# Idle products in planned gaps of the TensorE queue, with new planner constants, in a delta-rule attention and gated MLP kernel

## The chip, the cores and the metric

The kernel runs on one core of a Trainium2 chip. The metric is the device time of one execution in microseconds (us), as a median over runs. A profile is one execution, recorded instruction by instruction. Its engines are PE (TensorE matmul), PEld (TensorE weight load), DVE (VectorE), ACT (ScalarE), POOL (GpSimd) and SP (SyncE, whose queue issues the DMAs).

## What is computed

Three layers follow each other, all in float32 for a batch of 4 with 768 tokens: delta-rule attention over 8 heads of 48, a convolution-gated projection, and an MLP with a product over the tokens.

```python
for t in range(S):                                   # attention, state per head 48 x 48
    y[:, :, t] = einsum('bhd,bhde->bhe', q[:, :, t], state)
    v_old = einsum('bhde,bhd->bhe', state, kt)
    state = state + bt * einsum('bhd,bhe->bhde', kt, vt - v_old)
gate = sigmoid(causal depthwise conv of x, 5 taps)   # first gated layer, 384 wide
x = (gate * (x @ w_val)) @ w_out
h = gelu(x @ w_in); u, v = halves of h               # second layer, 1024 wide
v_s = einsum('ts,bsd->btd', w_sg, layernorm(v) * g_ln) + b_sg
out = x + (u * v_s) @ w_out2
```

## The kernel before

**Tiling.** The sequence is cut into 48 chunks of 64 tokens, 12 for each batch entry. `norm`, `keys`, `gram`, `base` and `merge` prepare the keys and the triangular inverses of sets of chunks; `base` is a recursion of some sixty small DVE operations for a set of eight chunks (tiles `X`, `tmp`). `seq(n)` carries the state through chunk n: PE forms `ps_q` and `ps_state`, and ACT and DVE read them back as pairs of float16 halves (`wh`). `attend(n)` forms the outputs (`ps_y`, `mh`, `ys`), which go to DRAM as `xd`. The MLP runs over tiles of 256 tokens: `front` (convolution, tile `a`), `value`, `hidden` (with the layer norm), `gates`, `mix`, `final`. Its PSUM banks are named `ps_mlp`. Nearly every product is three float16 products of halves. `load_weights`, `load_weights2` and `load_weights3` split the weights into halves on the chip, with exact float32 loads through the tile `wst` and float32 products with the identity `eye`.

**The order.** No loop writes the instruction order. Every call is recorded as an `Op` (which is why all instructions bear one line, L109), and `Program.in_order` then places all of them by list scheduling: it keeps a planned time for each engine, and lets each take, of the operations whose inputs are planned to be ready, the one with the highest weight. The weight is the length of the chain behind an operation, scaled by engine by the table `CHAIN`, plus an offset by stage (`STAGE`) and a term for its due chunk. The durations that the planner assumes come from `cost`. On the chip every engine then works through its queue strictly in the planned order, each instruction waiting on semaphores for its inputs. An instruction that stands early in a queue and has to wait holds up all behind it.

**TensorE in the planner.** `PE_WINDOW` and `PE_BUSY` say when the planner believes that TensorE runs at half clock; then it charges n / 1200 us for n columns in place of n / 2400. A product of a 64 x 64 block is charged at least 0.0255 us, and a change between blocks and full products `PE_CHANGE`.

**PSUM.** All eight banks are in use: `ps_a` one, `ps_m` three, and one each for `ps_b`, `ps_y`, `ps_q` and `ps_state`. The state uses 192 of the 512 columns of its bank.

Of the kernel before, what the change touches and what calls it, by code (L numbers as in the profile page):

```python
# [3 lines left out]

# [7 lines left out]
F32 = mybir.dt.float32  # L12
# [5 lines left out]
DRAM = bass.MemoryType.DRAM  # L18
# [3 lines left out]
class Op:  # L22


    def __init__(self, index, engine, method, call, kw):
        self.index, self.engine, self.method, self.call, self.kw = index, engine, method, call, kw
        self.before, self.after, self.stage, self.due = set(), [], None, 0
        self.ready = 0.0
        self.cost, self.time, self.port = cost(self)
        self.blocks = engine == "tensor" and kw["lhsT"].shape[0] == kw["lhsT"].shape[1] == 64  # L30


class Memory:
# [6 lines left out]
class Program:  # L40
# [7 lines left out]

    def __init__(self, tc):
        self.tc, self.ops, self.memory, self.masks, self.first = tc, [], {}, {}, []  # L50
        self.stage, self.due = None, 0
# [59 lines left out]
    def in_order(self):  # L111
        for op, m in self.first:
            op.before |= m.users
        for op in self.ops:
            assert all(o.index < op.index for o in op.before)
            op.left = len(op.before)
            for o in op.before:
                o.after.append(op)
        for op in reversed(self.ops):
            weight, wait = CHAIN[op.engine]  # L120
            op.chain = max((o.chain + (wait if o.engine != op.engine else 0.0) for o in op.after), default=0.0)
            op.chain += weight * (op.time + (op.cost + DMA_LATENCY + DMA_SEMAPHORE + reads(op) if op.engine == "sync" else 0.0))
# [12 lines left out]
        blocks = False  # L135

        def finish(op):
            for o in op.after:
                if o.engine != op.engine:
                    t = op.end + LATENCY[op.engine]  # L140
                elif op.engine == "tensor":
                    t = op.start
                else:
                    t = op.end + (LATENCY[op.engine] if op.engine == "sync" else 0.025)
                o.ready = max(o.ready, t)
                o.left -= 1
                if not o.left:
                    heappush(later[o.engine], (o.ready, o.index, o))

        while len(done) < len(self.ops) or waiting:  # L150
            t, e = min(((free[e] if now[e] else max(free[e], later[e][0][0]), i) for i, e in enumerate(ENGINES)
                        if (now[e] or later[e]) and not (waiting and e == "gpsimd")), default=(1e9, 0))
            if waiting and t >= held["vector"] + 0.02:
                op, waiting = waiting, None
                t = max(op.start, held["vector"])
                op.end = held["gpsimd"] = t + op.time
                free["gpsimd"] = t + op.cost
                finish(op)
                continue
# [19 lines left out]
            if e == "tensor" and op.blocks != blocks:  # L179
                blocks = op.blocks  # L180
                t += PE_CHANGE
            if e in ("vector", "scalar"):
                if e in last and drains(last[e], op):
                    t = max(t, last[e].start + last[e].time)
                last[e] = op
            op.start, used, time = t, op.cost, op.time
            done.append(op)
            if e == "vector":
                if op.port:
                    wait = max(0.0, held["gpsimd"] - t - 0.1)  # L190
                    wait += PORT_WAIT if wait > 0 else 0.0
                    used, time = used + wait, time + wait
                    held[e] = t + time - 0.05
            elif e == "gpsimd":
                if held["vector"] > t:
                    waiting = op
                    continue
                held[e] = t + time - 0.04
            elif e == "tensor":

                window, n = int(t / PE_WINDOW), int(np.prod(op.kw["out"].shape[1:])) * (mybir.dt.size(op.kw["rhs"].dtype) // 2) ** 2
                if busy.get(window - 1, 0) < PE_BUSY:
                    used = max(used, n / 1200)
                    time = max(time, used + 0.2)
                busy[window] = busy.get(window, 0) + n
# [7 lines left out]
            finish(op)  # L213
        return sorted(done, key=lambda op: (op.start, op.index))


# [33 lines left out]

DMA_QUEUE, DMA_SEMAPHORE = 8, 0.79

PE_WINDOW, PE_BUSY = 4096 / 1200, 3060

PE_CHANGE = 0.12

PORT_WAIT = 0.3

CHAIN = dict(tensor=(0.304, 0.508), scalar=(0.543, 0.071), vector=(2.092, 0.024), gpsimd=(2.017, 0.416), sync=(2.173, 0.387))


LATER = ("front", "value", "hidden", "gates", "mix", "final", "front0", "value0", "hidden0", "gates0", "mix0", "final0")
# [1 line left out]
DUE = dict(first=0.1, later=0.0534)  # L264


STAGE = dict(merge0=-0.2223, mix=0.3267, mix0=0.0197, gram0=-0.1735, load_weights2=-0.1156, seq0=0.0455, base0=0.0794, front0=0.1721, norm0=0.0229, load_weights3=0.0206, gates0=-0.0831, attend0=-0.0259, load_weights=0.0123)


def cost(op):  # L270
# [8 lines left out]
    far = n > 64 and any(step(a) > 8 for a in ins)  # L279
    if engine == "tensor":  # L280
        n *= 4 if mybir.dt.size(op.kw["rhs"].dtype) == 4 else 1
        t = max(0.0255, n / 1200 + 0.006 if step(op.kw["rhs"]) > 1 else n / 2400 + 0.0015)
        return t, t + 0.165, False
    if engine == "scalar":
        if apart:
# [4 lines left out]
        elif size == 4 and out.shape[0] == 32:  # L290
            t = 0.37
# [39 lines left out]

def reads(op):

    return DMA_READ if op.kw["in_"].space == DRAM else 0.0


def drains(op, after):

    p, q = (o.kw["out"].start_partition() for o in (op, after))
    return p != q and not (p < q and max(o.kw["out"].shape[0] for o in (op, after)) <= 64)  # L340


def step(ap):
# [15 lines left out]
def kernel(  # L359
# [150 lines left out]
    for x, t in [(0.0, eye32)] + [(x, const.tile([P, 128], F16, name=f"minus{i}")) for i, x in enumerate((1.0, SWG))]:  # L510
        nc.gpsimd.memset(t, 0.0)
        nc.gpsimd.affine_select(out=t, in_=t, pattern=[[1, 128]], compare_op=ALU.not_equal, fill=-1.0 / x if x else 1.0,
                                base=0, channel_multiplier=-1)
        minus[x] = t

    def hl_left(dst_hi, dst_lo, src, scale):

# [235 lines left out]
    def seq(n):  # L753
# [19 lines left out]
        hl_psum(we[:, 0], we[:, 1], pw, 1.0 / ST)  # L773
        if c < NC - 1:
            if c == 0:
                state["ps"] = ps_1.tile([P, PR, E], F32, name="ps_state", tag="s")
            pst = state["ps"]
            mmh(lambda h: pst[:, h, :], lambda x, h: kbd[x][:, h], lambda y, h: we[:, y, h], c == 0)
            hl_psum(we[0:EP, 2], we[0:EP, 3], pst[0:EP], 1.0 / SK)
# [415 lines left out]
```

## Time and profile before

| | |
|---|---|
| runs | 701.59, 702.41 and 706.77 us; median 702.41 us |
| profiled execution | 699.62 us; its span, from the first to the last instruction, is 697.9 us |
| busy in that span | PE 570.3 us (82%), DVE 529.2 (76%), ACT 400.6 (57%), POOL 175.1 (25%) |
| TensorE clock granted | mean 0.938 of full |

The span is read in stages, since the busy shares are averages over parts with different limits. Up to about 190 us the weights are split and the first eight chunks are worked; from there to 600 us the chunks and the MLP of earlier batch entries run side by side; in the last 98 us only the MLP of the last entry is left. Matmuls are pipelined and a busy PE is not one at its peak.

### The profile page before, as it was taken

What the parts mean: (1) busy time and instruction counts of PE and PEld (TensorE: products, weight loads), DVE (VectorE), ACT (ScalarE), POOL (GpSimd) and SP (SyncE); (2) the same over time, 40 slices, a digit from 0 to 9 for tenths busy, and PEclk for the clock granted to TensorE, in tenths of its full rate; (3) what the DMA queues carried; (4) which work ended last, traced back from release to release, by engine and by line L of the source; (5) the groups of instructions that cost most, each with busy time, mean ns of one, the idle gap of its engine ahead of it and who ended that gap; (6) DMA issues with size and microseconds to landing.
All of it is one profiled execution on the core that took longest, in us unless ns stands there. A gap on an engine that the chain in (4) does not pass through costs nothing. (4 is left out here: it accounts for less than half of the span.)

```text
span 697.9 us, 22453 instructions
## 1 busy us (share of the span) xinstructions
PE 570.3 (82%) x9255; PEld 463.4 (66%) x9255; DVE 529.2 (76%) x1346; ACT 400.6 (57%) x924; POOL 175.1 (25%) x186
## 2 busy tenths in 40 slices
PE   1428758755897678799999898999998999999897
PEld 1414436633775457578878686888886988977785
DVE  8697999899887987878988579989987657363222
ACT  9747756564767676585455646536566635334111
POOL 2413040063425163442302414201232100103000
PEclk9999859776699989999999999999999999999999
DMA  7743517898887887779798865567884585120121
GB/s 206 152 144 127 172 29 174 145 205 154 169 174 162 186 162 167 147 120 202 144 206 148 188 149 94 132 107 146 161 151 98 108 138 134 58 77 1 54 76 46
DMA packets 333110, 94.43 MB, mean 135 GB/s; under 512 B 274640, under 2 KB 323920, under 8 KB 333008
## 3 DMA queue, kind: packets, MB, share of 16 engines
q1 hardware_dynamic: 333008, 93.00, 62.3%
q8 instruction: 73, 1.20, 0.8%
q14 instruction: 29, 0.24, 0.1%
HBM read 51.81 MB, written 23.33 MB: 108 GB/s over the span
## 5 line engine op out<-in xcount | busy, mean ns | idle before, releaser
L109 PE MATMUL ps_mlp<-wg,vnh 128*128 128x256 f16 x864 | 103.4, 272 | 2.3 <-DVE ps_mlp L109 1.4
L109 PEld LDWEIGHTS <-kj 112*128 112x128 f16 (+1 forms) x1632 | 74.0, 100 | 42.9 <-issue 32.8
L109 PEld LDWEIGHTS <-vnh 128*128 128x128 f16 x864 | 82.9, 98 | 13.9 <-issue 2.4
L109 PEld LDWEIGHTS <-kc 64*64 64x64 f16 x1920 | 43.7, 123 | 39.4 <-DVE kc L109 18.5
L109 PE MATMUL ps_mlp<-wi,gvh 128*128 128x512 f16 x216 | 58.2, 380 | 6.9 <-DVE gvh L109 4.7
L109 DVE TENSOR_TENSOR X<-X,tmp 128x84 f32<-128x84 f32 (+12 forms) x156 | 61.2, 392 | 1.3
L109 PE MATMUL ps_mlp<-gvh,wi 128*128 128x256 f16 x432 | 60.5, 275 | 0.4 <-ACT u L109 0.4
L109 DVE TENSOR_TENSOR tmp<-X 128x84 f32<-128x84 f32 (+12 forms) x156 | 59.5, 382 | 1.3
L109 PE MATMUL ps_mlp<-gth,w 128*128 128x256 f16 x432 | 60.1, 272 | 0.0
L109 DVE SCALAR_TENSOR_TENSOR ps_mlp<-ps_mlp,gl,bs 128x256 f32<-128x256 f32 x48 | 22.9, 488 | 48.5 <-PE ps_mlp L109 47.5
L109 DVE SCALAR_TENSOR_TENSOR a<-x,cw,a 128x256 f32<-128x256 f32 x108 | 53.9, 546 | 4.0 <-ACT a L109 3.9
L109 PEld LDWEIGHTS <-ws 112*128 112x128 f16 (+1 forms) x1104 | 46.2, 100 | 14.7 <-issue 10.9
L109 PE MATMUL ps_mlp<-gvh,wo 128*128 128x256 f16 x324 | 48.9, 275 | 4.3 <-DVE gth L109 2.3
L109 PEld LDWEIGHTS <-m1p 128*128 128x128 f16 x1152 | 42.5, 98 | 14.6 <-issue 7.0
L109 PE MATMUL ps_mlp<-xh,wv 128*128 128x256 f16 x324 | 47.1, 275 | 4.9 <-ACT xh L109 2.3
L109 PE MATMUL ps_y<-mh,ws 128*128 128x64 f16 x576 | 43.1, 197 | 4.0 <-DMA ws<-wh 2.7
L109 PE MATMUL ps_y<-qh,ws 112*128 112x64 f16 x528 | 41.9, 197 | 5.2 <-DVE mh L109 5.1
L109 PEld LDWEIGHTS <-wi 128*128 128x128 f16 x432 | 39.8, 98 | 8.5 <-issue 3.0
L109 PEld LDWEIGHTS <-w 128*128 128x128 f16 x432 | 40.7, 97 | 4.5
L109 PEld LDWEIGHTS <-wo 128*128 128x128 f16 x342 | 32.5, 100 | 12.3 <-issue 6.5
L109 POOL TENSOR_TENSOR xh<-x,xh 128x780 f16<-128x780 f32 x12 | 20.3, 1694 | 76.9 <-ACT xh L109 76.9
L109 PE MATMUL ps_q<-wh,kj 112*128 112x48 f16 x528 | 29.4, 188 | 11.8 <-DMA kj<-keys_d 6.3
(156 smaller groups left out, 1370.2 us busy)
## 6 DMA issues: line engine op xcount, KB each, us to landing
keys_d<-kc SPq DMA_DIRECT2D x22, 512.0 KB, 3.9
ws<-wh SPq DMA_DIRECT2D x88, 128.0 KB, 3.9
kj<-keys_d SPq DMA_DIRECT2D x44, 256.0 KB, 5.7
wg<-wgd SPq DMA_DIRECT2D x12, 768.0 KB, 5.4
qf<-in_qt SPq DMA_DIRECT2D x24, 224.0 KB, 3.8
kf<-in_kn SPq DMA_DIRECT2D x12, 384.0 KB, 5.7
vf<-in_vn SPq DMA_DIRECT2D x24, 192.0 KB, 3.5
xd<-ys SPq DMA_DIRECT2D x48, 96.0 KB, 3.1
```

What stands on the lines that cost most here:

```text
L109: op.call()
```

## The change

Three things are changed together.

1. **Products of a constant.** One bank is now a tile `spare` that lives through the whole program; the state uses its columns 0 to 191. A function `filler` makes a product of the constant matrix `minus[1.0]` with itself into the columns 256 to 511: 128 x 256, or on a 64-partition half where blocks run. Nobody reads the result. When the planner is about to place a TensorE operation at a time more than 0.3 us after the engine's planned end, it puts such products into the planned gap, from its start on, until the 5 us before the operation hold 55% of the columns that a full clock would stream.
2. **The planner's account of TensorE.** Blocks cost 0.0162 us, a sliding window of 5.0 us with 4800 columns replaces the fixed one, the rule for half clock has other constants, and storing `xd` is charged 0.8 us more.
3. **New weights.** The tables `CHAIN` and `STAGE` have new numbers, so that the order of all engines is another one.

The core of the diff:

```diff
+            if e == "tensor":
+                if self.fill and t - free[e] > 0.3 and self.fill[1].end and free[e] > self.fill[1].end + 1.0:
+                    s = free[e]
...
+                    near = sum(n for x, n in ring if x >= t - PE_WINDOW)
+                    while near < FILL * 2400 * PE_WINDOW and s + 0.15 < t:
+                        for r in range(2 if blocks else 1):
+                            f = Op(len(self.ops) + len(done), "tensor", *self.fill[0](blocks, r))
+                            f.start, f.end = s, s + f.time
+                            done.append(f)
...
+                            s += f.cost
...
-                window, n = int(t / PE_WINDOW), int(np.prod(op.kw["out"].shape[1:])) * (mybir.dt.size(op.kw["rhs"].dtype) // 2) ** 2
-                if busy.get(window - 1, 0) < PE_BUSY:
-                    used = max(used, n / 1200)
-                    time = max(time, used + 0.2)
-                busy[window] = busy.get(window, 0) + n
+                n = columns(op)
+                while ring and ring[0][0] < t - PE_WINDOW:
+                    active -= ring.popleft()[1]
+                if active < PE_BUSY:
+                    used = max(0.0265 if op.blocks else 0.039, 2 * used - 0.006)
+                    time = used + 0.165
+                ring.append((t, n))
+                active += n
...
-PE_WINDOW, PE_BUSY = 4096 / 1200, 3060
+PE_WINDOW, PE_BUSY, FILL = 5.0, 4800, 0.55
...
-CHAIN = dict(tensor=(0.304, 0.508), scalar=(0.543, 0.071), vector=(2.092, 0.024), gpsimd=(2.017, 0.416), sync=(2.173, 0.387))
+CHAIN = dict(tensor=(0.235, 0.594), scalar=(0.543, 0.118), vector=(2.092, 0.02), gpsimd=(3.744, 0.378), sync=(2.173, 0.236))
...
+    spare = ps_1.tile([P, 512], F32, name="ps_state")
+
+    def filler(blocks, r):
+        rr = slice(r * C, (r + 1) * C) if blocks else slice(0, P)
+        one = minus[1.0][rr, rr]
+        kw = dict(out=spare[rr, 256:512].rearrange("p (a b) -> p a b", b=one.shape[1]), lhsT=one,
+                  rhs=one.unsqueeze(1).to_broadcast([one.shape[0], 256 // one.shape[1], one.shape[1]]), start=False, stop=False)
+        return "matmul", partial(nc.tensor.engine.matmul, **kw), kw
+
+    nc.tensor.matmul(**dict(filler(False, 0)[2], start=True))
+    nc.fill = filler, nc.ops[-1]
...
-                state["ps"] = ps_1.tile([P, PR, E], F32, name="ps_state", tag="s")
+                state["ps"] = spare[:, 0:PR * E].rearrange("p (u f) -> p u f", f=E)
```

TensorE's queue has 9717 matmuls now, and had 9231. The 486 more are products of the constant: 390 of 128 x 256 (one of them at the start of the program) and 96 of 64 x 256. They stand in 59 runs, of 1 to 45. Ahead of the last product `ps_y<-mh` of the eighth chunk stand 304 and 96, behind it 86, of which one stands in the second half of the program. Three places show the order.

**TensorE, the first float32 product of the weights.** The tile `wst` is a loaded piece of weight that DVE has to finish, `wo` a weight's upper half from ACT, `kc` keys. Before:

```order
L109 LDWEIGHTS kc_88
L109 MATMUL ps_q<-kc_88 64x64
L109 MATMUL ps_mlp<-wst,eye_104 128x384 [waits DVE_49,PE_49]
L109 LDWEIGHTS minus_105
L109 MATMUL ps_mlp<-wo,minus_105 128x384 [waits Activation_49]
```

Now 45 products stand between `kc` and `wst`, of which the last is shown, and then four:

```order
L110 LDWEIGHTS minus_105
L110 MATMUL ps_state<-minus_105 128x256
L110 MATMUL ps_mlp<-wst,eye_104 128x384 [waits DVE_49,PE_49]
L110 LDWEIGHTS minus_105
L110 MATMUL ps_state<-minus_105 128x256
L110 LDWEIGHTS minus_105
L110 MATMUL ps_state<-minus_105 128x256
```

The wait of the float32 product for DVE stays; what stands in the queue ahead of it is longer.

**TensorE, the state of the third chunk.** `ps_state` is the state that ACT and DVE read as `wh`; `ps_q` is the next chunk's first product with it. Before, three products of the weights stood between:

```order
L109 MATMUL ps_state<-wh_109,kj_92 128x48
L109 LDWEIGHTS wot
L109 MATMUL ps_mlp<-wih,wot 128x512
L109 LDWEIGHTS wot
L109 MATMUL ps_mlp<-wih,wot 128x512
L109 LDWEIGHTS wot
L109 MATMUL ps_mlp<-wih,wot 128x512
L109 LDWEIGHTS kj_92
L109 MATMUL ps_q<-wh_109,kj_92 128x48 [waits Activation_49]
```

Now five products of the constant stand there:

```order
L110 LDWEIGHTS minus_105
L110 MATMUL ps_state<-minus_105 128x256
L110 LDWEIGHTS minus_105
L110 MATMUL ps_state<-minus_105 128x256
L110 LDWEIGHTS minus_105
L110 MATMUL ps_state<-minus_105 128x256
L110 LDWEIGHTS minus_105
L110 MATMUL ps_state<-minus_105 128x256
L110 LDWEIGHTS minus_105
L110 MATMUL ps_state<-minus_105 128x256 [waits Activation_49]
L110 LDWEIGHTS kj_92
L110 MATMUL ps_q<-wh_110,kj_92 128x48
```

The wait for ACT's read of the state has moved from `ps_q` to the last of them, since both use one bank. In the other direction, five of ACT's 44 reads of `ps_state` and four of DVE's wait for a product of the constant that stands ahead of them, and not for the state's own last product.

**DVE, the last attention chunk.** `mh<-ps_y` is the last chunk's masked score on DVE, `a<-x,cw,a` the convolution of an MLP tile, `st` and `mv` the layer norm. Before:

```order
L109 SCALAR_TENSOR_TENSOR wh_109<-ps_q,wh_109 128x4x48
L109 BN_STATS st<-v 128x6
L109 BN_AGGR mv<-st 128x2
L109 SCALAR_TENSOR_TENSOR a<-x,cw,a 128x256 x9
L109 SCALAR_TENSOR_TENSOR ps_mlp<-ps_mlp,gl,bs 128x256
L109 SCALAR_TENSOR_TENSOR a<-x,cw,a 128x256 x3
L109 BN_STATS st<-v 128x6
L109 BN_AGGR mv<-st 128x2
L109 TENSOR_SCALAR va<-mv 128x2 x2
L109 SCALAR_TENSOR_TENSOR ps_mlp<-ps_mlp,gl,bs 128x256
L109 SCALAR_TENSOR_TENSOR ps_y<-ps_y,cmask 128x256
L109 TENSOR_TENSOR mh<-ps_y,mh 128x256
```

Now:

```order
L110 SCALAR_TENSOR_TENSOR ps_y<-ps_y,cmask 128x256
L110 SCALAR_TENSOR_TENSOR wh_110<-ps_q,wh_110 128x4x48
L110 TENSOR_TENSOR mh<-ps_y,mh 128x256
L110 BN_STATS st<-v 128x6
L110 BN_AGGR mv<-st 128x2
L110 SCALAR_TENSOR_TENSOR a<-x,cw,a 128x256 x7
```

The convolution of twelve operations, two layer-norm statistics and two reads of `mix` have moved behind the last `mh`. On TensorE 35 products of the MLP (18 of `wg,vnh` and 17 of `gvh,wi`) have moved behind the last `ps_y<-mh`.

## Rows read from the trace of the kernel before

**Rows 1.** The page: span, then busy us, share and instructions of each engine.

```profile
span 697.9 us, 22453 instructions
PE   570.3 (82%) x9255; PEld 463.4 (66%) x9255; DVE 529.2 (76%) x1346; ACT 400.6 (57%) x924; POOL 175.1 (25%) x186
```

**Rows 2.** Busy time by stage: stretch, length, engines' busy us, granted clock, DMA share, GB/s.

```profile
0.00:58.70 58.70, 21.41 (x378) 14.68 (x378) 46.88 (x126) 41.30 (x89) 17.15 (x37) 1.00 0.58 153
58.70:190.00 131.30, 92.19 (x1790) 65.01 (x1790) 118.95 (x294) 87.02 (x213) 37.08 (x34) 0.74 0.68 152
190.00:300.00 110.00, 84.91 (x1737) 67.27 (x1736) 87.58 (x242) 74.23 (x175) 43.83 (x43) 0.96 0.80 165
300.00:400.00 100.00, 91.17 (x1640) 78.74 (x1639) 82.74 (x226) 59.58 (x141) 29.21 (x26) 0.96 0.86 170
400.00:600.00 200.00, 192.20 (x2952) 163.54 (x2951) 162.12 (x399) 110.75 (x260) 37.55 (x35) 1.00 0.63 125
600.00:698.00 98.00, 88.46 (x773) 74.19 (x769) 30.93 (x62) 27.76 (x53) 10.29 (x11) 0.99 0.18 55
```

**Rows 3.** The same for the six stretches at half clock before 190 us.

```profile
65.50:68.90 3.40, 3.40 (x28) 1.75 (x21) 2.99 (x6) 2.49 (x8) 1.00 (x1) 0.50 0.42 165
...
sum 68.40, PE 45.50 PEld 32.73 DVE 61.36 ACT 35.33 POOL 26.36; mean PE 7.58 PEld 5.45 DVE 10.23 ACT 5.89 POOL 4.39
```

**Rows 4.** The same for the four stretches at half clock behind 190 us.

```profile
243.00:249.80 6.80, 3.51 (x74) 2.85 (x76) 6.14 (x22) 3.52 (x9) 4.09 (x6) 0.50 0.71 172
...
sum 17.00, PE 13.71 PEld 11.35 DVE 12.11 ACT 10.64 POOL 9.61; mean PE 3.43 PEld 2.84 DVE 3.03 ACT 2.66 POOL 2.40
```

**Rows 5.** DVE's waits from 58.7 to 190 us: waited for, us in total, times, longest.

```profile
DVE wh L109 <- ACT wh L109: 2.6, 3, 2.0
DVE wst L109 <- ACT wst L109: 2.2, 4, 1.0
DVE ps_q L109 <- PE ps_q L109: 1.9, 2, 1.4
DVE ps_y L109 <- PE ps_y L109: 1.1, 1, 1.1
```

**Rows 6.** TensorE's instructions in order of time: start, us, operation and count.

```profile
36.72 0.53 PE L109 MATMUL ps_mlp<-wo,minus 128*128 128x384 f16 x1
69.33 0.33 PE L109 MATMUL ps_mlp<-wih,minus 128*128 128x384 f16 x1
597.48 0.51 PE L109 MATMUL ps_y<-qh,kj 112*128 112x64 f16 x12
599.47 0.25 PE L109 MATMUL ps_y<-qh,ws 112*128 112x64 f16 x3
```

**Rows 7.** The chain that ended last: start, us, work and count.

```profile
600.36 11.91 PE ps_mlp L109 x109
649.82 30.93 PE ps_mlp L109 x280
```

**Rows 8.** TensorE's products by form from 297.6 to 301 us: count, busy us, mean ns, idle.

```profile
L109 PE MATMUL ps_mlp<-gvh,wi 128*128 128x256 f16 x9 | 2.1, 412 | 0.0
```

**Rows 9.** Instructions on the tile of the state: min, median and max ns, starts.

```profile
L109 PE MATMUL ps_state<-wh,kj x528: 182/183/248, 104.7 to 585.0; 128*128 128x48 f16 x176
```

**Rows 10.** TensorE's waits from 190 to 300 us.

```profile
PE ps_mlp L109 <- DVE gvh L109: 4.7, 1, 4.7
PE ps_q L109 <- ACT wh L109: 2.8, 2, 2.6
```

**Rows 11.** DVE's instructions by form from 590 to 600 us: count, busy us, mean ns, idle.

```profile
L109 DVE SCALAR_TENSOR_TENSOR a<-x,cw,a 128x256 f32<-128x256 f32 x12 | 4.9, 480 | 0.0
...
L109 DVE SCALAR_TENSOR_TENSOR ps_mlp<-ps_mlp,gl,bs 128x256 f32<-128x256 f32 x2 | 1.0, 491 | 0.6 <-PE ps_mlp L109 0.6
```

**Rows 12.** The DMAs of the tile `ws` from 586 to 602 us: durations, starts, us to landing.

```profile
L109 SPq DMA_DIRECT2D ws<-wh x4: 634/710/1090, 587.1 to 591.4; - x4
...
DMA to landing us min/median/max: 2.3/3.2/4.6
```

More of the change, by code (lines that the diff above doesn't have):

```diff
@@ L2 @@
 from functools import partial
+from collections import deque
 from heapq import heapify, heappop, heappush
@@ L27, in __init__ @@
         self.before, self.after, self.stage, self.due = set(), [], None, 0
-        self.ready = 0.0
+        self.ready = self.end = 0.0
+        self.blocks = engine == "tensor" and kw["lhsT"].shape[0] == kw["lhsT"].shape[1] == 64
         self.cost, self.time, self.port = cost(self)
-        self.blocks = engine == "tensor" and kw["lhsT"].shape[0] == kw["lhsT"].shape[1] == 64
 class Memory:
@@ L50, in __init__ @@
         self.tc, self.ops, self.memory, self.masks, self.first = tc, [], {}, {}, []
-        self.stage, self.due = None, 0
+        self.stage, self.due, self.fill = None, 0, None
         nc = tc.nc
@@ L134, in in_order @@
         held, waiting, last = dict(vector=0.0, gpsimd=0.0), None, {}
-        blocks = False
+        blocks, ring, active = False, deque(), 0.0
         def finish(op):
@@ L148, in finish @@
                     heappush(later[o.engine], (o.ready, o.index, o))
-        while len(done) < len(self.ops) or waiting:
+        count = 0
+        while count < len(self.ops):
             t, e = min(((free[e] if now[e] else max(free[e], later[e][0][0]), i) for i, e in enumerate(ENGINES)
@@ L158, in in_order @@
                 finish(op)
+                count += 1
                 continue
@@ L178, in in_order @@
                 op = heappop(now[e])[2]
-            if e == "tensor" and op.blocks != blocks:
-                blocks = op.blocks
-                t += PE_CHANGE
+            if e == "tensor":
+                if self.fill and t - free[e] > 0.3 and self.fill[1].end and free[e] > self.fill[1].end + 1.0:
+                    s = free[e]
+                    if op.blocks != blocks:
+                        blocks = op.blocks
+                        s += PE_CHANGE
+                    near = sum(n for x, n in ring if x >= t - PE_WINDOW)
[4 more added lines that the diff above has]
+                            done.append(f)
+                            n = columns(f)
+                            ring.append((s, n))
+                            active += n
+                            near += n * (s >= t - PE_WINDOW)
+                            s += f.cost
+                if op.blocks != blocks:
+                    blocks = op.blocks
+                    t += PE_CHANGE
             if e in ("vector", "scalar"):
@@ L199, in in_order @@
             elif e == "tensor":
-                window, n = int(t / PE_WINDOW), int(np.prod(op.kw["out"].shape[1:])) * (mybir.dt.size(op.kw["rhs"].dtype) // 2) ** 2
-                if busy.get(window - 1, 0) < PE_BUSY:
-                    used = max(used, n / 1200)
-                    time = max(time, used + 0.2)
-                busy[window] = busy.get(window, 0) + n
+                n = columns(op)
[5 more added lines that the diff above has]
+                ring.append((t, n))
+                active += n
             elif e == "sync":
@@ L213, in in_order @@
             finish(op)
+            count += 1
         return sorted(done, key=lambda op: (op.start, op.index))
@@ L251 @@
 DMA_QUEUE, DMA_SEMAPHORE = 8, 0.79
-PE_WINDOW, PE_BUSY = 4096 / 1200, 3060
-PE_CHANGE = 0.12
+PE_WINDOW, PE_BUSY, FILL = 5.0, 4800, 0.55
+PE_CHANGE, PE_BLOCK = 0.1, 0.0162
 PORT_WAIT = 0.3
-CHAIN = dict(tensor=(0.304, 0.508), scalar=(0.543, 0.071), vector=(2.092, 0.024), gpsimd=(2.017, 0.416), sync=(2.173, 0.387))
+CHAIN = dict(tensor=(0.235, 0.594), scalar=(0.543, 0.118), vector=(2.092, 0.02), gpsimd=(3.744, 0.378), sync=(2.173, 0.236))
 LATER = ("front", "value", "hidden", "gates", "mix", "final", "front0", "value0", "hidden0", "gates0", "mix0", "final0")
@@ L264 @@
 DUE = dict(first=0.1, later=0.0534)
-STAGE = dict(merge0=-0.2223, mix=0.3267, mix0=0.0197, gram0=-0.1735, load_weights2=-0.1156, seq0=0.0455, base0=0.0794, front0=0.1721, norm0=0.0229, load_weights3=0.0206, gates0=-0.0831, attend0=-0.0259, load_weights=0.0123)
+STAGE = dict(merge0=-0.2278, mix=0.4968, mix0=0.0197, gram0=-0.3653, load_weights2=-0.2397, seq0=0.0455, base0=0.01, front0=0.0691, gates0=-0.0985, attend0=-0.0259, load_weights=0.0147, gram=-0.0326, value=0.0939, attend=0.043, load_weights3=0.0199, final=-0.0062, keys0=0.0755)
 def cost(op):
@@ L281, in cost @@
         n *= 4 if mybir.dt.size(op.kw["rhs"].dtype) == 4 else 1
-        t = max(0.0255, n / 1200 + 0.006 if step(op.kw["rhs"]) > 1 else n / 2400 + 0.0015)
+        t = (PE_BLOCK if n <= 64 else n / 4800 + 0.0015) if op.blocks else max(0.0255, n / 1200 + 0.006 if step(op.kw["rhs"]) > 1 else n / 2400 + 0.0027)
         return t, t + 0.165, False
@@ L332, in reads @@
 def reads(op):
-    return DMA_READ if op.kw["in_"].space == DRAM else 0.0
+    return DMA_READ if op.kw["in_"].space == DRAM else 0.8 if "xd" in op.kw["out"].tensor.name else 0.0
 def drains(op, after):
@@ L340, in drains, with columns @@
     return p != q and not (p < q and max(o.kw["out"].shape[0] for o in (op, after)) <= 64)
+def columns(op):
+    n = int(np.prod(op.kw["out"].shape[1:])) * (mybir.dt.size(op.kw["rhs"].dtype) // 2) ** 2
+    return n * 0.6 if op.blocks else n
 def step(ap):
```

## The prediction

> **What bounds the kernel now.** I read the stages first, then the stretches at half clock, then who waits for whom. The page gives PE 570.3 us and DVE 529.2 us of a span of 697.9 us [rows 1], but the two are full in different stages. Up to 190 us DVE is the bound: from 58.7 to 190 us it is busy 118.95 of 131.3 us, while PE is busy 92.19 us at a mean clock of 0.74 [rows 2]. From 190 to 400 us neither is full (PE 84.91 of 110 and 91.17 of 100, DVE 87.58 and 82.74). From 400 to 600 us PE is busy 192.2 of 200 us, and in the last 98 us it is busy 88.46 us while DVE has 30.93 us of work [rows 2]. So a saving counts in full only where it is on DVE's path early, or on PE's path late.
>
> The half clock lies mostly where PE is not the bound. Six stretches before 190 us hold 68.4 us, with PE busy 45.5 us and DVE busy 61.36 us [rows 3]; four behind it hold 17 us, with PE busy 13.71 us [rows 4]. Before 58.7 us the clock column reads 1.00, and yet a product of 384 columns took 0.53 us at 36.7 us and 0.33 us at 69.3 us [rows 6]; the difference is that of a half and a full clock, so the first weight products were slow too and the column has no record there.
>
> I sum against the profiled execution, 699.6 us, whose span is 697.9 us. The median of the three runs is 702.4 us, 2.8 us more, so the sum is carried over to that median.
>
> **Part 1, what the clock gives back.** PE busy at half clock can at best halve. A stream of 256-column products takes 30.93 / 280 = 0.110 us each at full clock [rows 7] and 2.1 / 9 = 0.23 us at half [rows 8].
> - To 58.7 us: DVE is busy 46.88 us [rows 2] and finishes `wst` before PE can use it. From 0 to -1.5 us; I take -0.5, near nothing, because the waiting engine is PE.
> - 58.7 to 190 us: half of 45.5 us is 22.8 us of PE time, but DVE is idle only 68.4 - 61.36 = 7.0 us in those stretches [rows 3], and a faster PE can give no more than that while DVE's own work stays. Of DVE's waits in this stage 1.9 + 1.1 us are for PE itself and 2.6 us for ACT's `wh`, which stands behind PE [rows 5]: 5.6 us, of which a faster clock takes back somewhat under half. From 0 to -7.0 us; I take -2.5.
> - Behind 190 us: half of 13.71 us is 6.9 us [rows 4]. The products of the constant stand there nearly all ahead of 300 us, so only the stretch at 243 us (PE busy 3.51 us) is surely reached; the other three depend on where the new order leaves gaps. From 0 to -6.9 us; I take -3.0, some 1.5 us from the first and a third of the rest.
>
> The TensorE page of the Trainium skill (TensorE: Matmul & The Clock Gate, Part 1) says that the ramp penalty is under 1% of a typical kernel's span and need not be modelled closely. The rows differ: by half of 59.2 us, up to 4% of this span is PE time lost to the clock, although most of it is behind DVE. [...]
>
> **Part 2, what the products cost.** There are 390 of 256 columns and 96 halves on 64 partitions. The first are 390 x 0.110 = 43 us at full clock. No row shows 256 columns on 64 partitions: between 0.055 us, if two halves run side by side, and 0.110 us each, so 5 to 11 us; I take 5, as the planner puts them in pairs, and the difference lies where PE idles. They are hidden where PE really waits. Ahead of the eighth chunk's last product (188 us in this trace) stand about 33 + 5 = 39 us of them, and PE is idle 37.3 + 39.1 = 76.4 us to 190 us [rows 2]. Behind it stand 86 x 0.110 = 9.5 us against 25.1 us of idle time from 190 to 300 us [rows 2], in waits such as the 4.7 us for `gvh` and 2.6 us for `wh` [rows 10]. Each stands in front of real work in a strict queue: what is issued when PE is late, and not its input, is added in full. From 0 to +9.5 us behind 190 us, and ahead of it up to a tenth of 39 us on the path; I take +2.0, some 18 products.
>
> **Part 3, the shared bank.** Nine reads of the state wait for a product of the constant ahead of them. With four such products, each read starts up to 4 x 0.110 = 0.44 us later than behind `ps_state`'s own 183 ns [rows 9], and `ps_q` and the next chunk are queued behind it. From 0 to 9 x 0.44 = +4 us; I take +0.5, since ACT and DVE have other work first in most places and the planner had placed the reads later anyway.
>
> **Part 4, the new order.** It moves nearly everything a little. At the end of the attention DVE has 12 operations `a` of 480 ns (4.9 us busy), two `mix` reads (1.0 us) and the two layer-norm statistics less ahead of the last `mh` [rows 11]. In this trace the last `ps_y` starts at 599.5 us and its first half at 597.5 [rows 6]. Its other input, the DMA of `ws`, is issued at 591.4 us at the latest and lands at most 4.6 us later, at 596.0 [rows 12]. So the last attention can come at most 599.5 - 596.0 = 3.5 us earlier, however much DVE is relieved; after that the landing is the next thing that is late. On PE 35 x 0.110 = 3.8 us of products have moved behind it, into the last stage, where PE is idle 98 - 88.46 = 9.5 us [rows 2] and, in the end, streams without a pause (280 products in 30.93 us [rows 7]). If these products find idle time, the 3.5 us stay; if not, nothing stays. In the other direction the sequence of chunks starts later in DVE's queue: with this trace's durations laid along both orders, some 5 us (an estimate) more of DVE's work stands ahead of the `rh` of the second to the twelfth chunk than before, and in a DVE-bound stage that could stay to the end. From -9 us (all of DVE's relief) to +5 us; I take -3.5.
>
> **Sum.** -0.5 - 2.5 - 3.0 + 2.0 + 0.5 - 3.5 = -7.0 us: 692.6 us against the profiled execution, and 702.4 - 7.0 = 695.4, say 695 us, against the median.
>
> **Rivals.**
> - *The products stand in the way (slower).* Place: TensorE's queue from 190 to 300 us, PE busy 77% there. If the 86 products are issued when PE is late, they add 9.5 us, a tenth of the 39 us ahead adds 4, and the reads of the state the 4 us of part 3: +17.5 against -6 of the clock, some 713 us. It decides from about 85 products on the path (9.5 us against the 9.5 us that the clock and the order give). For it speaks that the gaps are planned, not measured; against it that PE waits longer than the products last in every stage to 300 us.
> - *DVE is the bound anyway (no change).* The clock gives back only DVE's waits for PE, 3.0 us [rows 5], the three stretches behind 297 us stay, the products cost 2 and the last attention is taken back by the 3.8 us moved behind it: -1 to 0, 702 us. The busy share of 118.95 in 131.3 speaks for it [rows 2].
> - *The new order packs better (much faster).* From 190 to 600 us PE is idle 25.1 + 8.8 + 7.8 = 41.7 us [rows 2]. A planner that charges blocks and clock as the chip does leaves fewer unplanned waits; a third of this is 14 us, with the 6 us of the clock 20 us: 682 us. For it speaks that neither engine is full from 190 to 400 us; against it that the order of the stages is almost the same.
> - *The clock does not rise.* Then the gaps hold products at 0.23 us each, 90 us, more than PE's 76.4 us of idle time there, and it ends like the first rival or worse. A product as wide as that streams at full clock behind 600 us, so I give it little.
>
> **Chances.** Forecast (688 to 699 us) 0.40; better packing (676 to 688) 0.21; no change (699 to 707) 0.19; in the way, with the last rival (707 to 722) 0.20. The range must leave out 2 in 10: the lower half of the better packing (0.11) and the upper half of the slower cases (0.10) go, so 683 to 711. The likeliest one's own range is 688 to 699. A measurement of this kernel tells about 1%, 7 us, from no change. Faster by over 1% (below 695.4) is half of the forecast and all of the better packing, 0.41; within 1% the other half and no change, 0.39; slower 0.20.
>
> **What would show it.** Right: a granted clock of 1.00 from about 35 us to 300 us, products `ps_state<-minus` where PE idled; DVE still over 85% busy from 58.7 to 190 us, with waits for PE below 1.5 us; the last `ps_y` near 594 us. Part 2 is wrong if PE is busy and its real products come later than in this trace from 190 to 300 us, part 3 if ACT waits at `wh` for products of the constant over 2 us in all, part 4 if the last `ps_y` is not earlier or the last stage grows by more than it gains. The forecast falls if DVE shows long waits that are not here now, or if the eighth chunk is not done by 186 us.

## The result and the profile after

The kernel with the change takes 698.43 us in the median of 20 runs (689.67 to 702.63), the kernel before 702.61 us beside it (698.51 to 707.65). The ratio is 0.991 with a 95% interval of [0.9881, 0.9939]: about 0.9% faster, 4.2 us by the medians and some 6 us by the ratio. I had forecast 695 us, 7 us less than before.

The profiled execution of the changed kernel took 699.59 us, with a span of 697.9 us. That is the span which the profile of before happens to have [rows 1]: this pair of profiles shows what moved, and no gain. The gain stands in the medians alone, which is why the split below rests on timed runs.

The page of the kernel after, with the group of the products of the constant (busy us, mean ns, idle time before):

```profile
span 697.9 us, 23412 instructions
...
PE 603.8 (87%) x9741; PEld 491.8 (70%) x9741; DVE 525.0 (75%) x1346; ACT 402.5 (58%) x924; POOL 174.9 (25%) x186
...
L110 PE MATMUL ps_state<-minus 128*128 128x256 f16 (+1 forms) x486 | 63.3, 287 | 7.7 <-ACT wh L110 4.5
```

TensorE is busy 33.5 us more than in [rows 1], and the other engines within 5 us of what they were. The same six stages as in [rows 2], with the granted clock in the third column from the right:

```profile
0.00:58.70 58.70, 34.53 (x559) 27.30 (x560) 44.77 (x123) 42.03 (x90) 16.70 (x37) 0.94 0.56 152
58.70:190.00 131.30, 104.50 (x1910) 75.72 (x1910) 113.17 (x287) 85.27 (x201) 36.68 (x35) 0.94 0.62 145
190.00:300.00 110.00, 90.33 (x1775) 70.93 (x1772) 88.60 (x240) 71.65 (x169) 40.52 (x41) 0.97 0.79 161
300.00:400.00 100.00, 93.31 (x1679) 81.29 (x1676) 86.87 (x235) 63.76 (x149) 32.56 (x31) 0.98 0.87 175
400.00:600.00 200.00, 192.94 (x3078) 163.13 (x3077) 161.17 (x402) 111.70 (x266) 37.96 (x34) 1.00 0.67 130
600.00:698.00 98.00, 88.20 (x759) 73.48 (x756) 30.44 (x62) 28.10 (x53) 10.43 (x12) 0.99 0.17 53
```

From 58.7 to 190 us the clock is 0.94 in place of 0.74. Seven stretches at half clock are recorded now, and ten stand in [rows 3] and [rows 4]; the first of the seven and their sum:

```profile
37.60:44.50 6.90, 6.21 (x23) 4.07 (x24) 5.81 (x23) 2.52 (x6) 0.00 (x0) 0.51 0.39 119
...
sum 34.10, PE 32.28 PEld 21.94 DVE 27.37 ACT 18.45 POOL 6.46; mean PE 4.61 PEld 3.13 DVE 3.91 ACT 2.64 POOL 0.92
```

The first of the seven lies ahead of 58.7 us, where the profile of before has no record of the clock. Behind 58.7 us, where both have one, 34.1 - 6.9 = 27.2 us are left at half clock with PE busy 26.07, where before had 68.4 + 17.0 = 85.4 us with PE busy 59.2. So the change does to the clock most of what it says.

What it does to the length shows when both kernels are cut at the same work and not at the same microsecond. The three parts are: to the end of the eighth chunk's `ys` on ACT, from there to the end of the last `ps_y` on PE, and the rest. Before:

```profile
0.00:189.50 189.50, 113.10 (x2164) 79.55 (x2165) 165.33 (x418) 127.83 (x300) 54.22 (x71) 0.82 0.64 152
189.50:600.40 410.90, 369.18 (x6334) 310.07 (x6333) 332.94 (x867) 245.46 (x575) 110.58 (x104) 0.98 0.73 147
600.40:697.90 97.50, 88.06 (x760) 73.80 (x758) 30.93 (x62) 27.36 (x52) 10.29 (x11) 1.00 0.18 56
```

After:

```profile
0.00:201.70 201.70, 148.54 (x2694) 109.94 (x2695) 167.41 (x436) 134.81 (x311) 54.05 (x72) 0.94 0.61 148
201.70:595.90 394.20, 362.98 (x6253) 304.76 (x6253) 323.94 (x840) 238.22 (x560) 109.69 (x102) 0.99 0.76 150
595.90:697.90 102.00, 92.30 (x796) 77.15 (x794) 33.68 (x72) 29.48 (x55) 11.12 (x13) 0.99 0.17 53
```

The first part is 12.2 us longer, the middle 16.7 us shorter, the last 4.5 us longer, which makes zero in this pair. DVE's operations show that work changed its place: 18 more in the first part, 27 fewer in the middle, 10 more in the last (one lies across a border).

### The profile page after: what moved, and what is told of

It is laid out like the page before. It is cut to its first block, busy times and chain, and to the rows that moved or that the text cites. A ratio compares the mean times of both kernels' runs of the same rounds, so it can differ in the third digit from the quotient of the medians.

```text
span 697.9 us, 23412 instructions
## 1 busy us (share of the span) xinstructions
PE 603.8 (87%) x9741; PEld 491.8 (70%) x9741; DVE 525.0 (75%) x1346; ACT 402.5 (58%) x924; POOL 174.9 (25%) x186
## 4 chain that ended last, share of the span: by engine, by line
PE 41%; DVE 22%; DMA 17%; ACT 8%; issue 6%; SPq 5%; POOL 1%; ACTq 0%; POOLq 0%; DVEq 0%
PE ps_mlp L110 29%; DMA ws<-wh 5%; SPq L110 5%; PE ps_y L110 4%; DVE X L110 4%; DVE tmp L110 3%; PE pk L110 2%; PE ps_q L110 2%; DMA qf<-in_qt 2%; PE ps_state L110 2%; DVE a L110 1%; PE ps_b L110 1%; DMA m1p<-gx 1%; DVE m1p L110 1%; DVE wh L110 1%
## 5 line engine op out<-in xcount | busy, mean ns | idle before, releaser
L110 PEld LDWEIGHTS <-kj 112*128 112x128 f16 (+1 forms) x1632 | 67.2, 98 | 28.2 <-issue 19.5
L110 PE MATMUL ps_state<-minus 128*128 128x256 f16 (+1 forms) x486 | 63.3, 287 | 7.7 <-ACT wh L110 4.5
L110 PEld LDWEIGHTS <-kc 64*64 64x64 f16 x1920 | 40.5, 116 | 35.7 <-DVE kc L110 15.2
L110 PE MATMUL ps_mlp<-gvh,wi 128*128 128x256 f16 x432 | 58.7, 273 | 0.4 <-ACT u L110 0.4
L110 PEld LDWEIGHTS <-minus 128*128 128x128 f16 (+1 forms) x510 | 44.8, 104 | 19.1 <-issue 8.8
L110 PEld LDWEIGHTS <-ws 112*128 112x128 f16 (+1 forms) x1104 | 41.7, 97 | 17.2 <-issue 11.4
L110 PE MATMUL ps_mlp<-gvh,wo 128*128 128x256 f16 x324 | 45.1, 272 | 4.4 <-DVE gth L110 2.4
L110 PEld LDWEIGHTS <-m1p 128*128 128x128 f16 x1152 | 38.0, 96 | 10.1 <-issue 4.4
L110 PE MATMUL ps_y<-mh,ws 128*128 128x64 f16 x576 | 37.6, 193 | 7.0 <-DMA ws<-wh 5.8
L110 PE MATMUL ps_mlp<-xh,wv 128*128 128x256 f16 x324 | 41.7, 272 | 0.0
L110 PE MATMUL ps_y<-qh,ws 112*128 112x64 f16 x528 | 37.7, 193 | 4.3 <-DVE mh L110 4.3
```

What stands on the lines that cost most here:

```text
L110: op.call()
```

## The experiments

The theory after these rows: the products of the constant give a few us net, and the new order by itself gives nothing, because what it takes out of the middle it puts in front and behind. The rival: the gain is the order's, and the products with their clock change nothing, since DVE is the bound early.

Ratios are to the kernel before, timed on the same chip in between. Three sets of runs are told apart, since before itself took 702.6 us in the first comparison (above), 695.0 us in the second and 698.9 us in the third; three experiments (the late products dropped, every product twice, the mixed offsets) and the second profile of before come from a set on one more chip, with 696.9 us. The changed kernel was not timed in that set, so the times of those three are compared with it across chips.

**The order without the products.** Every engine's queue as in the changed kernel, and the products left out as the program is issued.

```diff
             for op in ops:
-                op.call()
+                if op.index < len(self.ops):
+                    op.call()
```

> The changed kernel's order of every engine, with the 485 products of the constant left out at the last moment (only the first one at the start of the program is issued); nothing that is read later is changed. Theory (the clock gives it): without them the mean granted clock falls back from 0.97 to 0.94 or below and the time goes to 702 us (699 to 706), the old kernel's. Rival A (the new order gives it): 698 us, the changed kernel's, at the lower clock. Rival B (the products stand in the way): faster than the changed kernel, 690 to 695 us.

Measured: 697.75 us (691.13 to 701.37), ratio 1.0025 [0.9993, 1.0057], clock 0.909. The changed kernel again, beside it:

> The changed kernel once more, on the same chip as the kernels beside it, as their measure and for a second profile: 695 to 700 us, 0.991 of the old kernel; a mean granted clock of 0.96 to 0.98. If the spread from run to run comes from where the half-clock stretches fall, this profile shows them at other places than the first one.

Measured: 693.97 us (690.41 to 697.59), ratio 0.9969 [0.994, 0.9998], clock 0.98. Before itself took 695.04 us here, so both kernels came out faster than expected, and the changed one gains less than the 0.991; but the pair decides: the order alone gains nothing, and with the products it is 3.8 us faster. Its three parts, without the products:

```profile
0.00:197.70 197.70, 120.26 (x2295) 83.30 (x2296) 166.83 (x436) 135.18 (x311) 54.22 (x72) 0.77 0.61 151
197.70:593.00 395.30, 358.69 (x6168) 301.83 (x6168) 323.14 (x840) 238.59 (x560) 109.52 (x102) 0.96 0.75 150
593.00:694.50 101.50, 92.03 (x796) 77.08 (x793) 33.69 (x72) 29.48 (x55) 11.15 (x13) 1.00 0.17 53
```

And with them:

```profile
0.00:197.90 197.90, 146.14 (x2694) 108.19 (x2695) 167.24 (x436) 134.71 (x311) 54.11 (x72) 0.96 0.62 151
197.90:592.00 394.10, 363.22 (x6253) 305.69 (x6253) 324.66 (x840) 238.39 (x561) 109.79 (x102) 0.99 0.76 150
592.00:693.50 101.50, 92.17 (x796) 77.14 (x793) 33.65 (x72) 29.59 (x55) 11.15 (x13) 1.00 0.18 53
```

All that moved between the parts is there without the products: the late eighth chunk (197.7 us), the short middle, the long last part. The late chunk is the order's doing. The middle of the new order holds 358.69 us of PE work in place of 369.18, 10.5 us less, and 36.6 us of idle time in place of 41.7; of the 10.5 us, 7.2 lie in the first part now (PE 120.26 against 113.10) and 4.0 in the last (92.03 against 88.06). The 5 us of idle time are no firm gain: a second profile of the kernel before (696.91 us) has 407.40 us in the middle with PE busy 370.52, so 36.9 us idle.

The clock is recorded from the start in this pair. In the order alone PE is busy 77.46 us at half clock, and with the products 26.14 us. These two profiles differ by only 1.0 us in length (694.5 and 693.5), and the first part is not shorter with the products (197.9 against 197.7 us): they show the clock that the products give back, but not the place of the 3.8 us.

> The old kernel once more, for a profile of the same chip as the kernels beside it. 1.00 of itself; half clock for 60 to 70 us up to 190 us and at other places than in its first profile; chunk 1 near 116 us and the last chunk's output near 600 us, and some 97 us from there to the end. If the new order's last stage is longer by the 3.8 us of products moved into it, the changed kernel has 101 us there.

**The products without the order.** Before's queues, with 347 products put into the planned gaps by the same 55% in 5 us, under the old account and weights.

```diff
+            if e == "tensor":
+                if self.fill and t - free[e] > 0.3 and self.fill[1].end and free[e] > self.fill[1].end + 1.0:
+                    s = free[e]
+                    near = sum(n for x, n in ring if x >= t - 5.0)
+                    while near < 0.55 * 2400 * 5.0 and s + 0.15 < t:
...
+                            fills.append(f)
...
-        return sorted(done, key=lambda op: (op.start, op.index))
+        return sorted(done + fills, key=lambda op: (op.start, op.index))
```

> The old kernel's order of every engine, to the instruction, with 347 products of the constant put into the gaps that the old planner sees on TensorE, by the same rule of 55% in 5 us; old account, old weights. Theory (the clock gives it): the mean granted clock rises to about 0.97 and the time falls by some 4 us, to 698 us. Rival A (the new order gives it): 702 us, since DVE is the bound where the clock is low. Rival B (the products stand in the way): above 704 us, more than the old kernel, because the old planner's gaps are the less true ones.

Measured: 692.12 us (689.8 to 699.22), ratio 0.998 [0.9942, 1.0019], clock 0.962. The eighth chunk ends at 183.8 us, 6 us earlier than in before, but the ratio can't be told from no change, though the medians are 2.9 us apart. Its middle:

```profile
183.80:593.50 409.70, 375.02 (x6380) 315.27 (x6379) 334.10 (x868) 244.86 (x574) 111.38 (x104) 0.98 0.74 147
```

It is 409.7 us long against 410.9 and 407.4 in the two profiles of before: what is won by the eighth chunk reaches the end in part at most. A second profile (the third comparison below) has the chunk done at 185.6 us and a middle of 411.3 us.

**The late products alone dropped.** The 86 behind the eighth chunk's last `ps_y<-mh` are not issued.

```diff
+            chunk = [op for op in ops if op.stage in ("attend", "attend0") and op.engine == "tensor" and "mh" in op.kw["rhs"].tensor.name]
+            mark = ops.index(chunk[12 * 8 - 1])
+            for i, op in enumerate(ops):
+                if op.index < len(self.ops) or i < mark:
+                    op.call()
```

> The changed kernel's order with the products of the constant issued only up to the eighth chunk's last product: 400 of 486, the 86 behind it left out. Theory (the clock gives the gain, a part of it behind 190 us): half clock comes back between 200 and 270 us and the time rises by 1 to 3 us over the changed kernel. Rival A (only the early products count, DVE sets the pace later): the same time within 1 us. Rival B (the products behind 190 us stand in the way): 2 to 5 us faster than the changed kernel.

Measured: 694.55 us (690.97 to 697.38), ratio 0.9974 [0.9945, 1.0004]. The clock did fall where they are gone, to 0.86 from 190 to 300 us, from 0.97, 0.95 and 0.94 in three profiles of the changed kernel:

```profile
190.00:300.00 110.00, 85.86 (x1649) 67.19 (x1644) 88.52 (x237) 73.27 (x173) 42.73 (x42) 0.86 0.83 163
```

The middle is no longer for it, 391.7 us, against 394.2, 394.1 and 393.1 us in the three profiles of the changed kernel:

```profile
198.20:589.90 391.70, 358.59 (x6168) 301.54 (x6168) 323.08 (x840) 238.08 (x559) 109.39 (x102) 0.96 0.76 150
```

So the traces show no price of the lower clock in that stage, net of the products' own cost. The times don't settle it: the ratio is close to the changed kernel's of the second comparison (0.9969), but lies 0.6 and 0.8 points above its ratios of the other two (0.991 and 0.9891).

**Every product twice.**

```diff
+                if op.index >= len(self.ops):
+                    op.call()
```

> The changed kernel's order with every product of the constant issued twice, 971 in all, some 48 us of TensorE time more. Theory (they lie in real waits with room): 0 to 4 us slower than the changed kernel, clock 0.98 or more. Rival B (they stand in the way): 10 us slower or more, in proportion to the 48 us, and by that the single ones cost as much.

Measured: 702.93 us (700.57 to 705.25), ratio 1.0096 [1.0062, 1.0131], with the fullest clock of all, 0.993. The two lines of products:

```profile
L110 PE MATMUL ps_state<-minus 128*128 128x256 f16 (+1 forms) x486 | 100.6, 274 | 6.9 <-ACT wh L110 3.7
...
L112 PE MATMUL ps_state<-minus 128*128 128x256 f16 (+1 forms) x485 | 99.9, 273 | 0.0
```

The first part of that kernel:

```profile
0.00:204.90 204.90, 174.02 (x3093) 139.72 (x3094) 168.42 (x436) 134.48 (x311) 55.16 (x72) 0.99 0.59 146
```

(The times of neighbouring matmuls overlap in the rows, so both lines read higher than what they add.) Against the kernel without the late products, on the same chip, the time is 702.93 - 694.55 = 8.4 us longer; against the changed kernel of the second comparison it is 9.0 us, 19% of some 48 us of products (an estimate, from 0.110 us for each 256 columns). 6.7 us of the 8.4 show in the first part (204.9 against 198.2 us). The theory's 0 to 4 us is missed, and the result lies near rival B in size though far from the whole 48 us. Products in planned gaps are not free; the first set fills most of what is really idle.

**The weights.** The changed kernel with the old tables `CHAIN` and `STAGE`, which makes 580 products (the line of `STAGE` is replaced in the same way):

```diff
-CHAIN = dict(tensor=(0.235, 0.594), scalar=(0.543, 0.118), vector=(2.092, 0.02), gpsimd=(3.744, 0.378), sync=(2.173, 0.236))
+CHAIN = dict(tensor=(0.304, 0.508), scalar=(0.543, 0.071), vector=(2.092, 0.024), gpsimd=(2.017, 0.416), sync=(2.173, 0.387))
```

> The changed kernel's account and products with the old tables CHAIN and STAGE: a third order, drawn by neither. Theory (the clock gives it, the order little): 697 to 701 us. Rival A (the new weights give it): 703 us or more, as the old weights were fitted to the old account.

Measured: 702.49 us (700.65 to 703.31), ratio 1.0093 [1.0057, 1.0129]: short of rival A's 703 us, and nearer to it than to the theory's 701. And with the old offsets for the first batch's stages and the weight loads alone, which was to bring the first chunks forward:

> The changed kernel with the old offsets for the stages of the first batch entry and the weight loads, and the new ones for the rest. Theory (the new order's early lateness of some 7 us reaches the end): chunk 1 earlier than in the changed kernel and 2 to 5 us faster than it. Rival (the lateness is taken back by 400 us, since PE and DVE have other work to do): the same as the changed kernel within 2 us, or slower as any other order may be.

Measured: 704.69 us (702.62 to 709.52), ratio 1.0131 [1.0082, 1.0179]. Its first chunk ended at 116.6 us and its eighth at 194.7, earlier than in the three profiles of the changed kernel (201.7, 197.9 and 195.9), and its time is some 10 us longer. Its middle:

```profile
194.70:601.70 407.00, 370.19 (x6336) 308.84 (x6335) 341.04 (x852) 243.01 (x566) 108.76 (x103) 0.99 0.75 146
```

The middle is 12.8 us longer than the changed kernel's 394.20, with 7.2 us more of PE work in it, 5.6 us more of PE's idle time, and 17 us more of DVE's (341.04 for 852 operations against 323.94 for 840; why they take longer was not followed up), while its last part, 101.9 us, is the new order's long one. Two things follow from the pair. How early the eighth chunk ends does not decide the time; the work and the waits that are left behind it count as well. And an order drawn for another account, or mixed from two, came out 0.9 and 1.3% above before: the new weights are worth 8.5 us to the changed kernel (702.49 against 693.97 us, in one set), and with them the order only comes back to what the old one had under the old account.

**The same comparison on another chip.** The changed kernel, the order alone and the products alone, once more.

> The changed kernel again, beside the kernel before. Two comparisons so far gave 0.991 and 0.997 of before. If the difference between them belongs to the cores (before ran at 702.6 us in the one, 695.0 us in the other), this one should fall near one of the two, by the time that before has here: about 0.991 where before takes 702 us, about 0.997 where it takes 695 us. If it is only the runs of before that differ, after should stand within 692 to 699 us whatever before does.

> After's order of every engine, with its products of the constant not issued. Theory: the order alone gains nothing (the first time it was 1.0025 of before), so 0.999 to 1.006, and over after by 3 to 4.5 us. Rival: the order alone carries the larger gain of the first comparison, then 0.993 to 0.997 and within 2 us of after.

> Before's order of every engine, with 347 products in its gaps. Theory: where before runs slowly (702 us), the missing clock is what makes it slow, and the products give back more here: 0.992 to 0.995. Rival: the products are worth the same everywhere, 0.998 as the first time.

| | second comparison | third comparison |
|---|---|---|
| before | 695.04 us | 698.93 us |
| changed kernel | 693.97, 0.9969 [0.994, 0.9998] | 692.04, 0.9891 [0.9856, 0.9927] |
| order alone | 697.75, 1.0025 [0.9993, 1.0057] | 696.76, 0.9974 [0.9941, 1.0007] |
| products alone | 692.12, 0.998 [0.9942, 1.0019] | 696.06, 0.995 [0.9918, 0.9982] |

All three ratios are lower here, by 0.3 to 0.8 points. Neither of my two ways to read the first difference holds: 0.9891 came with a before of 698.9 us, not 702. The order alone, 0.9974, falls between the theory's range and the rival's, and the products alone, 0.995, at the theory's edge, though before did not run slowly. A shift that all three kernels share lies mostly in the runs of before. The rows within a column agree better: from the order alone to the changed kernel it is -3.8 and -4.7 us. In the third comparison the two do not even overlap (689.36 to 692.38 against 693.10 to 703.71).

## Why the prediction was right, and where it was not

**The sum.** I forecast -7.0 us; the three comparisons gave medians 4.2, 1.1 and 6.9 us lower, by the ratios 0.9, 0.3 and 1.1%. The direction and the range were right. By the medians the forecast's size was met in the third comparison alone, and the parts show which term was too large.

**Parts 1 to 3 together: -3.5 forecast, -3.8 and -4.7 us measured** (the changed kernel against its own order without products). It is shown that the products give the gain: with the same order they raise the clock from 0.909 to 0.98 and take some 4 us off. That they give it by way of the clock is argued, since no run changes the clock without them. For it speaks that within the changed kernel's own runs a higher mean clock goes with a shorter time (correlation -0.73, -0.70 and -0.86 over the runs of the three comparisons); in the order alone there is no steady relation (0.13 and -0.58).

Which of my three items of the clock carries it is open. The third (-3.0 behind 190 us) is not to be seen: without the 86 late products the clock there fell to 0.86, and the middle was no longer. But the first two (-3.0 together) are not to be seen at their place either: in the two pairs of profiles the first part is 0.2 us longer and 1.6 us shorter with the products (197.9 and 197.7 us; 195.9 and 197.5 us).

Gross gain and cost can't be parted by these runs. If the first set cost what the second did, part 2 would be 8 to 9 us and not the 2 that I took; nothing shows which. That some 4 us are all that comes of the 51 us of half-clock PE time that went away in this order (77.46 - 26.14) fits [rows 2] and [rows 3]: DVE is the bound early. It still is: 113.17 of 131.3 us, 86%. Its waits in that stage:

```profile
DVE gd L110 <- ACT gd L110: 3.4, 2, 2.7
DVE wh L110 <- ACT wh L110: 2.9, 5, 1.0
...
DVE wh L110 <- PE ps_state L110: 0.9, 1, 0.9
DVE ps_y L110 <- PE ps_y L110: 0.9, 1, 0.9
```

The longest waits are for ACT, as before; those for PE missed the mark that I named (under 1.5 us): they fell from 3.0 us to 2.3, with a third row of 0.5 us for `ps_q`.

The Trainium skill's page TensorE: Matmul & The Clock Gate (Part 1) puts the ramp penalty under 1% of a typical kernel's span. It says so of the first products of a kernel, and the half clock here comes back after gaps all along the span. So I was wrong to set the 4% of the prediction against it, and the 0.54% and 0.68% that the products gave back here, by the medians, do not bear it out either.

**Part 3 (+0.5 us): no larger cost shows.** ACT's reads of the state wait as long as before. The rows of those who waited for the tile `ps_state` (us, times), before:

```profile
ACT wh L109: 15.4, 15
...
DVE wh L109: 5.4, 7
```

And after:

```profile
ACT wh L110: 14.8, 16
DVE wh L110: 9.7, 11
PE ps_state L110: 5.0, 5
```

DVE's reads wait 4.3 us longer, but that is the new order's: without the products the two profiles have 8.7 and 8.3 us there. The shared bank shows the other way round: five times a product of the constant waited on PE until ACT or DVE had read the state, 5.0 us in all. The longest, on PE's timeline:

```profile
215.58 0.58 PE L110 MATMUL ps_state<-minus 128*128 128x256 f16 x2 [3.44 <-ACT wh L110]
215.96 0.52 PE L110 MATMUL ps_q<-wh,kj 112*128 112x48 f16 x8
```

The real product behind it needed the same `wh`, so this wait would have been there anyway. In all, PE waited 6.0, 8.3 and 6.8 us for the readers of the state in three profiles of the changed kernel, and 5.5 and 3.1 us in two of the order alone: a few us of PE's waits at most, and no run shows how much of them reaches the end.

**Part 4 (-3.5 us) is the step that failed.** The order alone measured 1.0025 and 0.9974, zero in the mean and not clear of zero in either. The -3.5 us, a ratio of 0.995, lies outside the first interval and just inside the second, and the ratios of one kernel move by half a percent between sets; so the traces have to say what became of it. I had given the condition myself: "If these products find idle time, the 3.5 us stay; if not, nothing stays", and took the first branch. It was the second. The bound "at most 3.5 us" did not hold: the DMA of `ws` was itself issued earlier, at 588.7 us at the latest in place of 591.4.

```profile
L110 SPq DMA_DIRECT2D ws<-wh x4: 590/597/659, 579.9 to 588.7; - x4
```

The last `ps_y` ends 600.4 - 595.9 = 4.5 us earlier in the first pair, and the last part is 102.0 against 97.5 us. PE's busy time there grew by 92.30 - 88.06 = 4.2 us, as the 35 moved products say (3.8 us), and its idle time stayed, 9.7 against 9.4 us. Its longest waits there are the same too, 2.3 to 2.4 us each for `u` (ACT) and `gth` (DVE) in either kernel; the work moved there has not slipped into them. The same holds in every kernel with this order (101.5 to 102.0 us), with and without products.

**The mark of the eighth chunk was a wrong mark.** I wrote that the forecast falls if it is not done by 186 us. It was done at 201.7, 197.9 and 195.9 us in three profiles, and the forecast held. Without products it is as late (197.7 and 197.5), so they are not what makes it late; DVE and PE had done 18 operations and 7.2 us of later work ahead of it, which the middle is then spared. A milestone says something on the end only with the work that is left behind it.

**The marks of the clock.** "1.00 from 35 to 300 us" did not come: 0.94, 0.94 and 0.97. The gaps were planned, and where the chip is later than the plan PE idles on behind the products: at 38.29 us the float32 product waits 2.7 us for `wst`, in the stretch from 37.6 to 44.5 us that is recorded at half clock. The inference that the clock column has no record before 58.7 us in the profile of before is borne out twice. In the changed kernel the product of 384 columns took 0.53 us at 40.55 us, inside that stretch, and 0.33 us at 44.91 us, behind it. And in the order alone, in its run of the third comparison, the first stage is recorded, at 0.70:

```profile
0.00:58.70 58.70, 21.26 (x395) 14.57 (x395) 46.37 (x126) 43.28 (x93) 17.45 (x37) 0.70 0.56 152
```

So the mean clocks of the two profiles of before, 0.938 and 0.945, count that stage as full and are too high. With 0.70 in the first 58.7 us they would be about 0.913 and 0.920 (an estimate from that row), much like the order alone.

**The rivals.** *In the way* is what happens from the second set on (+1.0% over before); one set stays below that. *DVE is bound anyway* was right for the order, and some 4 us short for the products. *Packs better* is excluded for the order alone. *The clock does not rise* is excluded by 0.98 against 0.909.

**What stays open:** why the kernel before, and with it every ratio, differs by half a percent between sets of runs; which gaps earn the 4 us, and whether by the clock alone; and whether the products earn as much in the old order, where 0.998 and 0.995 average to -0.35%, 2.4 us, and the medians give 2.9 us both times. No version beat the changed kernel clearly.

## What to carry over

Fill planned gaps of TensorE only up to what is really idle: here the first set gained 4 us and a second one lost 8 to 9, at the best clock of all. To judge a new order, cut both traces at the same work and write down for each part its length, PE's busy time and PE's idle time: what one part is spared may stand in another, as here 10.5 us of the middle's PE work in front of and behind it. Test a change of clock and a change of order apart, by leaving the idle products out of the very same order; two profiles of single runs (697.9 us both here) can hide the gain altogether.

## What the runs showed of the hardware

Between kernels the granted clock and the time part ways. The mean clocks 0.909, 0.98 and 0.993 belong to 697.75 us (order alone), 693.97 us (changed) and 702.93 us (doubled, on another chip). Within the changed kernel's own runs the two go together, as told above. Where the gap filling was dropped behind the eighth chunk, the clock from 190 to 300 us was 0.86 in place of 0.94 to 0.97, and the middle was no longer (391.7 us against 393.1 to 394.2). A profile may hold no record of the clock at its start, and the column reads 1.00 there: in both profiles of before it does so to 58.7 us, where the order alone is recorded at 0.71 and 0.70. And the places of the half-clock stretches move from run to run of one kernel: two profiles of the changed kernel have 0.97 and 0.94 from 190 to 300 us, and the eighth chunk 5.8 us apart (201.7 and 195.9 us).
